# RWKV-6 recurrence and a token-mixing MLP on one core: twelve of the loads split into 120 and 8 partitions

## The chip, the cores and the metric

The kernel runs on 1 core of one Trainium2 chip. The metric is the device time of one execution in microseconds (us); lower is better. Before the change three runs gave 105.36, 105.78 and 107.31 us, median 105.78.

## What is computed

Inputs `r`, `k`, `v`, `w` have 4 batches, 8 heads, 768 tokens and 48 channels in float32; `u` is 8 x 48. The first stage is a recurrence per batch and head, the second a mixing of all tokens of a batch:

```
for t in range(768):
    cur = outer(u * k[t], v[t])
    y[t] = r[t] @ (state + cur)
    state = w[t][:, None] * state + outer(k[t], v[t])
x = y as (batch, 768, 8 * 48 = 384)
wq, wk = x @ w_q, x @ w_k                       # 384 -> 64
mixed = (wq @ wk.T / sqrt(64)) @ x
out = relu(mixed) @ w_out                       # 384 -> 384
```

## The kernel before

The work is cut into 12 units of 256 tokens, three for each batch (`unit(n, batch)`, L429). A unit holds two chunks of 128 tokens; the recurrence is done chunk by chunk as matrix products, and only the 48 x 48 states are carried from chunk to chunk.

**Loads.** For each unit SyncE's queue (SP) issues one transfer of 384 KB for each of `w`, `k` and `r` (tiles `wg`, `kg`, `rg`), and for `v` (`vg`) in the first nine units; the last batch (`WHOLE`, L233) gets its `v` by four transfers of another shape (`vw`, `load_whole`, L296). `load` (L291) lays two neighbouring tokens in one partition: 128 partitions, in each 8 heads times 96 floats, so 8 runs of 384 bytes a partition. Each kind has a ring of four buffers (`RINGS`, L257). The weights of the second stage come by three transfers in the middle of the loads.

**A unit's steps.** ScalarE (ACT) takes the logarithm of `w` into `lw` (L453); GpSimd (POOL) or ACT casts `kg` and `rg` to bf16 (`k`, `r`, L463); POOL casts `vg` (`v`, L556). TensorE (PE) sums the logarithms with a triangular matrix (`CM`, `cw`), ACT makes the exponentials `ep` and `en` (L491, L496). PE transposes `k` and `r`; a copy of the former is `ks`, and VectorE (DVE) multiplies to `RT` (L531) and `qT` (L522), POOL or DVE to `KT` (L539). PE puts `v` into token order (`vp`, with the permutation `PM`; a copy is `VB`). PE makes the products of a chunk (`A`), DVE masks them (`AM`, L608), POOL makes the diagonal term `Vd` (L588), PE the state (`sn`; `SB`, L654) and the outputs (`yi`, `ya`), DVE joins them to `X` (L712). Transposed (`XT`) they go into the products `QK`. At the end of a batch PE makes `T`, `mx` and `fp`, copies give `TS`, `MX` and `os`, and SP stores (L824). All matmuls have line L240.

**The order of the work.** A class `Plan` holds all steps. Each has a fixed rank (`RANK`, L165); `order()` (L80) lets each engine's steps stand in the order of their ranks and merges the engines' lists by planned durations, with which it also assigns PSUM banks. A load's issue, its time on the wire and its landing are planned by `plan.dma` (L73), called for loads at L441. SP's steps stay in the order of their ranks whatever happens on the chip, and so do the other engines' steps; waits go by semaphores. The transfers use eight landing semaphores in turn, and a transfer waits for the one that used its semaphore before, eight transfers earlier.

With the order in the program, the loads of SP from the eleventh on are: kg n3, wg n3, rg n2, wg n4, vg n2, vg n3, rg n3, kg n4, kg n5, three weights, rg n4, wg n5, rg n5, vg n4, kg n6, wg n6, vg n5, wg n7, kg n7, rg n6, kg n8, vg n6, vg n7, vg n8, wg n8, rg n7, rg n8, rg n9, and the rest ("kg n3" is the tile `kg` of unit 3).

Of the kernel before, what the change touches and what calls it, by code (L numbers as in the profile page):

```python
# [17 lines left out]
def view(t, off, dims, p0=0, pn=128):  # L18

    base = t[ds(p0, pn), ds(off, 1)]  # L20
    return dataclasses.replace(base, ap=[list(base.ap[0])] + [list(d) for d in dims])
# [12 lines left out]
class Plan:  # L34
# [12 lines left out]
    def add(self, key, engs, fn, after=(), buf=None, reads=(), lag=None, mode=0, behind=None):  # L47
        e = next(iter(engs)) if len(engs) == 1 else next(self.alt, "")
        e = e if e in engs else next(iter(engs))
        if lag is None:  # L50
            lag = 260 if e == "E" else 80
        s = dict(key=key, engs=engs, eng=e, dur=engs[e], fn=fn, lag=lag, mode=mode, rank=0,
                 behind=behind, after=list(after), buf=buf, reads=list(reads), i=len(self.steps))
        if buf is not None:
            if buf.filler is None:
                buf.filler = s
                s["fill"] = buf.kind
                if behind is None:
                    s["behind"] = self.last.get(buf.kind)
                if buf.kind in self.rings:  # L60
                    self.last[buf.kind] = s
            else:
                s["fill"] = None
                if behind is None:
                    s["behind"] = buf.filler
        else:
            s["fill"] = None
        for b in reads:
            b.readers.append(s)
        self.steps.append(s)  # L70
        return s
# [133 lines left out]
def kernel(  # L205
# [12 lines left out]
    nc = tc.nc  # L218
    B, H, S, D = r.shape
    C = 128  # L220
    U = 2 * C
# [3 lines left out]
    D2 = 2 * D  # L225
# [5 lines left out]
    N = B * NU  # L231

    WHOLE = (3,)  # L233

    SHIFT = 25
    MU = -SHIFT * math.log(2.0) / C
# [11 lines left out]
    def const(shape, dtype, name):  # L248
# [15 lines left out]
        QK=(2, QW, BF16), TS=(2, DM, BF16), vw=(2, NCH * DM, F32))  # L264
    if not WHOLE:
        del RINGS["vw"]
# [21 lines left out]
    gv = const([C, 1], F32, "gv")  # L288
    gk = const([C, 1], F32, "gk")

    def load(b, i, tl, ap):  # L291
        nc.sync.dma_start(  # L292
            out=view(tl, 0, [[D2, H], [1, D2]]),
            in_=ap[b, :, ds(i * U, U)].rearrange("h (p j) d -> p h (j d)", j=2))

    def load_whole(b, q, tl):  # L296
        n_ = H // 2 * NCH
# [62 lines left out]
    def ring(kind):  # L360
        b = Buf(kind)
        b.tile = tiles[kind][used[kind] % RINGS[kind][0]]
        used[kind] += 1
        return b
# [7 lines left out]
    def at(b, dtype=F32):  # L372
        x = PS[:, ds(b.bank * 512, 1024 if b.kind == "w" else 512)]
        return x if dtype == F32 else x.bitcast(dtype)

    def copies(cols, half=False, by=False):

        return {"A": (270 if by else 170) + int(cols * 0.835),
                "D": (210 if by else 150) + int(cols * (0.523 if half else 1.045))}

    def copy(e, o, i, by=None):
        if e == "A":
            if by is None:
                nc.scalar.copy(o, i)  # L384
            else:
                nc.scalar.activation(o, i, ACT.Copy, bias=0.0, scale=by)
        else:
            x = nc.vector if e == "D" else nc.gpsimd
            if by is None:
                x.tensor_copy(o, i)  # L390
            else:
                x.tensor_scalar_mul(o, i, by)
# [36 lines left out]
    def unit(n, batch):  # L429
        b, i = divmod(n, NU)  # L430
# [4 lines left out]
        fine = each if split else both  # L435
        whole = b in WHOLE

        g = {}
        for name, ap in (("wg", w), ("kg", k), ("rg", r)) + (() if whole else (("vg", v),)):
            g[name] = ring(name)  # L440
            g[name + "L"] = plan.dma((name, n), 570, 1190 + 250 * (n == 0 and name == 'kg') + 250 * (n > 2),  # L441
                                     lambda e, ap=ap, x=g[name].tile: load(b, i, x, ap),
                                     buf=g[name])[1]
        if whole and i == 0:
            batch["vw"] = ring("vw")
# [41 lines left out]
        for cs in fine:  # L487
# [11 lines left out]
            x = add(("ep", n, cs[0]), {"A": 190 + int(w_ * 0.837)}, f_ep, [cws], ep, [cw])  # L499
# [27 lines left out]
        for cs in fine:  # L527
# [8 lines left out]
            def f_KT(e, cs=cs, n4=n4):  # L536
# [3 lines left out]
            x = add(("RT", n, cs[0]), {"D": 150 + int(n4 * C * 0.524)}, f_RT,  # L540
                    [rTs] + [eps[c] for c in cs], RT, [rT, ep])
# [43 lines left out]
        for cs in fine:  # L585
# [5 lines left out]
            x = add(("Vd", n, cs[0]), {"P": 185 + 646 * len(cs)}, f_vd, [VBs, dds], Vd, [VB, dd])  # L591
# [22 lines left out]
        for cs in ([(0,)] if final else fine):  # L614
# [4 lines left out]
            x = add(("kb", n, cs[0]), {"E": 225 * len(cs)}, f_kb, [KTs[c] for c in cs], kb, [KT])  # L619
# [4 lines left out]
            x = add(("kd", n, cs[0]), copies(DM * len(cs), True, True), f_kd, [x], kd, [kb])  # L624
# [46 lines left out]
        for side in sides:  # L671
# [5 lines left out]
            def f_yi(e, side=side, cs=cs, first=not yis[cs[0]]):  # L677
# [3 lines left out]
                for hp in range(NP):  # L681
# [4 lines left out]
            x = add(("yi", n, *side[0]), {"E": 54 * len(side) + 60 * bool(yis[cs[0]])}, f_yi,  # L686
                    [RTs[c] for c in cs] + [oldss[c] for c in cs] + yis[cs[0]], ys[cs[0]],
                    [RT] + [olds[c] for c in cs], mode=1)
# [18 lines left out]
        for p, cs in enumerate(each if end else both):  # L707
# [42 lines left out]
            if not end:  # L750
                def f_qk(e, f_wk=f_wk, f_wq=f_wq):
# [3 lines left out]
                x = add(("QK", n), copies(384), lambda e, qk=qk: copy(  # L755
                    e, QK.tile[:, ds(i * QS, 384)], at(qk)[:, ds(0, 384)]), [qs], QK, [qk])
# [79 lines left out]
    for n in range(N):  # L836
        if n % NU == 0:
            batch = {"k": [], "q": [], "x": []}
        unit(n, batch)
# [42 lines left out]
```

## Time and profile before

| what | value |
|---|---|
| median of 3 runs | 105.78 us (105.36 to 107.31) |
| the profiled execution: span from its first to its last instruction | 104.4 us |
| the profiled execution's own time beyond the span | not recorded; the median is 1.4 us above the span |
| mean granted TensorE clock | 0.984 |
| read from HBM, written to it | 19.66 MB, 4.72 MB |
| loads of 384 KB: median time from issue to landing, wg, kg, rg, vg | 5.4, 5.9, 5.9, 5.8 us |

The page of the profile has the busy time of each engine (PE TensorE matmuls, PEld its weight loads, DVE VectorE, ACT ScalarE, POOL GpSimd, SP SyncE's queue), the span in 40 slices, the DMA queues (q1 is SP's queue of loads and stores, q8 and q14 fetch instructions), the chain of work that ended last, and the costliest groups of instructions. "A <- B" in the waits says that A stood idle until B had finished. In a timeline a line has start, duration, engine, line, operation, out<-in, and in brackets the engine's idle time before it and what ended it. A wait for several semaphores is put down to the one that came last by the profile.

### The profile page before, as it was taken

What the parts mean: (1) busy time and instruction counts of PE and PEld (TensorE: products, weight loads), DVE (VectorE), ACT (ScalarE), POOL (GpSimd) and SP (SyncE); (2) the same over time, 40 slices, a digit from 0 to 9 for tenths busy, and PEclk for the clock granted to TensorE, in tenths of its full rate; (3) what the DMA queues carried; (4) which work ended last, traced back from release to release, by engine and by line L of the source; (5) the groups of instructions that cost most, each with busy time, mean ns of one, the idle gap of its engine ahead of it and who ended that gap; (6) DMA issues with size and microseconds to landing.
All of it is one profiled execution on the core that took longest, in us unless ns stands there. A gap on an engine that the chain in (4) does not pass through costs nothing.

```text
span 104.4 us, 3964 instructions
## 1 busy us (share of the span) xinstructions
PE 93.2 (89%) x1651; PEld 69.4 (66%) x1652; DVE 84.4 (81%) x140; ACT 80.6 (77%) x122; POOL 69.3 (66%) x80
## 2 busy tenths in 40 slices
PE   5999899766998999999999899999999998999910
PEld 2356488544777786767886776887888596866500
DVE  6669996995789979979999889999899699695320
ACT  6348988759879869999999886899897954855830
POOL 6607666979998828959995699999975973000000
PEclk9999999999589999999999999999999999999999
DMA  1999999999999988999999799999993056004791
GB/s 26 296 324 325 325 318 234 309 290 237 301 342 295 246 228 206 303 254 243 310 294 256 195 264 276 244 179 172 292 349 137 0 220 238 0 9 181 295 359 72
DMA packets 56803, 24.65 MB, mean 236 GB/s; under 512 B 54480, under 2 KB 55632, under 8 KB 56784
## 3 DMA queue, kind: packets, MB, share of 16 engines
q1 hardware_dynamic: 56224, 24.19, 84.3%
q8 instruction: 13, 0.21, 0.8%
q10 hardware_dynamic: 560, 0.20, 0.7%
q14 instruction: 6, 0.05, 0.1%
HBM read 19.66 MB, written 4.72 MB: 234 GB/s over the span
## 4 chain that ended last, share of the span: by engine, by line
PE 74%; DMA 6%; POOL 5%; DVE 5%; issue 3%; ACT 2%; SPq 1%; POOLq 0%; DVEq 0%
PE PS L240 74%; DMA vg<-in_v_dram 6%; DVE KT L539 2%; POOL KT L539 2%; POOL v L556 2%; POOL Vd L588 1%; ACT ep L491 1%; ACT MX L396 1%; DVE RT L531 1%; DVE AM L608 1%; SPq L292 1%; DVE qT L522 1%; ACT os L384 0%; DVE Z L306 0%; POOL r L463 0%
## 5 line engine op out<-in xcount | busy, mean ns | idle before, releaser
L608 DVE TENSOR_TENSOR AM<-PS,US 128x1024 bf16<-128x1024 f32 x24 | 29.3, 1219 | 3.4 <-PE PS L240 3.2
L539 POOL TENSOR_TENSOR KT<-ks,en 128x1024 bf16<-128x1024 bf16 (+1 forms) x11 | 20.5, 1864 | 3.6 <-DVE ks L390 3.4
L588 POOL TENSOR_TENSOR Vd<-VB,dd 128x768 bf16<-128x768 bf16 (+1 forms) x14 | 18.1, 1294 | 1.3 <-ACT dd L384 1.2
L712 DVE SCALAR_TENSOR_TENSOR X<-PS,gx,Vd 128x768 bf16<-128x768 f32 (+1 forms) x13 | 12.4, 952 | 2.8 <-POOL Vd L588 1.4
L240 PEld LDWEIGHTS <-KT 48*128 48x128 bf16 (+1 forms) x272 | 10.9, 97 | 5.2 <-issue 2.4
L496 ACT ACTIVATE en<-PS 128x1024 bf16<-128x1024 f32 (+1 forms) x14 | 12.6, 898 | 2.0 <-PE PS L240 2.0
L491 ACT ACTIVATE ep<-PS 128x1024 bf16<-128x1024 f32 (+1 forms) x14 | 12.7, 919 | 1.3 <-ACT XT L384 0.6
L453 ACT ACTIVATE lw<-wg 128x768 bf16<-128x768 f32 x12 | 10.2, 848 | 4.5 <-DMA wg<-in_w_dram 4.4
L240 PE MATMUL PS<-wo,MX 128*128 128x384 bf16 x72 | 13.3, 326 | 0.0
L463 POOL CAST k<-kg 128x768 bf16<-128x768 f32 x11 | 9.0, 825 | 3.3 <-DMA kg<-in_k_dram 3.3
L384 ACT COPY os<-PS 128x768 f32<-128x768 f32 (+1 forms) x13 | 8.6, 680 | 2.5 <-PE PS L240 2.2
L463 POOL CAST r<-rg 128x768 bf16<-128x768 f32 x9 | 7.5, 835 | 4.3 <-DMA rg<-in_r_dram 2.3
L556 POOL CAST v<-vg 128x768 bf16<-128x768 f32 x9 | 7.4, 825 | 3.6 <-DMA vg<-in_v_dram 3.6
L240 PE MATMUL PS<-RT,KT 48*128 48x128 bf16 x192 | 9.7, 221 | 0.0
L240 PEld LDWEIGHTS <-MX 128*128 128x128 bf16 x72 | 6.5, 98 | 4.1 <-issue 0.3
L531 DVE TENSOR_TENSOR RT<-PS,ep 128x1024 bf16<-128x1024 bf16 (+1 forms) x14 | 8.4, 607 | 0.8 <-PE PS L240 0.5
L396 ACT ACTIVATE MX<-PS 128x768 bf16<-128x768 f32 (+1 forms) x11 | 8.2, 755 | 0.7 <-PE PS L240 0.6
L522 DVE TENSOR_TENSOR qT<-PS,ks 128x1024 bf16<-128x1024 bf16 x12 | 8.2, 681 | 0.4 <-issue 0.4
L240 PE MATMUL PS<-Z 128*128 128x512 bf16 x20 | 7.4, 511 | 1.2 <-DVE uT L309 1.2
L384 ACT COPY XT<-PS 128x768 bf16<-128x768 bf16 (+1 forms) x9 | 6.9, 765 | 2.0 <-PE PS L240 2.0
L240 PE MATMUL PS<-ID,r 128*128 128x128 bf16 x96 | 7.7, 226 | 0.4 <-POOL r L463 0.3
L240 PE MATMUL PS<-VB,AM 128*128 128x48 bf16 x192 | 7.9, 184 | 0.1
(83 smaller groups left out, 201.1 us busy)
## 6 DMA issues: line engine op xcount, KB each, us to landing
wg<-in_w_dram SPq DMA_DIRECT2D x12, 384.0 KB, 5.4
kg<-in_k_dram SPq DMA_DIRECT2D x12, 384.0 KB, 5.9
rg<-in_r_dram SPq DMA_DIRECT2D x12, 384.0 KB, 5.9
vg<-in_v_dram SPq DMA_DIRECT2D x9, 384.0 KB, 5.8
out_dram<-os SPq DMA_DIRECT2D x9, 384.0 KB, 3.0
vw<-in_v_dram SPq DMA_DIRECT2D x4, 288.0 KB, 6.2
out_dram<-os SPq DMA_DIRECT2D x5, 192.0 KB, 2.7
wof<-in_moe_w_out_dram SPq DMA_DIRECT2D x1, 576.0 KB, 5.4
```

The lines of the kernel that those rows point to most:

```text
L240: return nc.tensor.matmul(o, l, rr, start=start, stop=stop, skip_group_check=True, is_transpose=trans)
L384: nc.scalar.copy(o, i)
L453: nc.scalar.activation(view(lw.tile, 0, [[64, H], [512, 2], [1, D]]), view(g["wg"].tile, 0, [[D2, H], [D, 2], [1, D]]), ACT.Ln, bias=0.0, ...
L463: op(view(o.tile, 0, [[64, H], [512, 2], [1, D]]), view(g[src].tile, 0, [[D2, H], [D, 2], [1, D]]))
L491: nc.scalar.activation(view(ep.tile, cs[0] * NP * EW + 66, [[EW, NP * len(cs)], [-65, 2], [1, 64]]), at(cw)[:, ds(cs[0] * 512, w_)], ACT.E ...
L496: nc.scalar.activation(en.tile[:, ds(cs[0] * 512, w_)], at(cw)[:, ds(cs[0] * 512, w_)], ACT.Exp, bias=0.0, scale=-1.0)
L531: nc.vector.tensor_tensor(view(RT.tile, cs[0] * 512, [[C, n4], [64, 2], [1, 64]]), view(at(rT, BF16), cs[0] * 512, [[C, n4], [64, 2], [1, ...
L539: x.tensor_tensor(KT.tile[:, cols], ks.tile[:, cols], en.tile[:, cols], ALU.mult)
L556: v16s = add(("v16", n), {"P": 826}, lambda e: nc.gpsimd.tensor_copy(view(v16.tile, 0, [[D, H], [DM, 2], [1, D]]), view(g["vg"].tile, 0, [ ...
L588: nc.gpsimd.tensor_tensor(Vd.tile[:, cols], VB.tile[:, cols], view(dd.tile, cs[0] * H, [[1, len(cs) * H], [0, D]]), ALU.mult)
L608: AMs[c] = add(("AM", n, c), {"D": 1221}, lambda e, c=c, A=A: nc.vector.tensor_tensor(view(AM[c].tile, 0, [[C, 8], [1, C]]), view(at(A), 0 ...
L712: nc.vector.scalar_tensor_tensor(view(X.tile, (2 * i + c0) * DM, [[DM, nc_], [1, DM]]), view(at(y), 0, [[512, nc_], [1, DM]]), gx, view(Vd ...
```

## The change

In the loads of `kg` and `rg` of units 3 to 8, twelve loads, partitions 0 to 119 go by one transfer and partitions 120 to 127 by a second one issued right behind it on the same queue. The bytes and the destination are the same; the planner's durations and ranks are unchanged, and so is the order of all other instructions on every engine. SP issues 12 transfers more, and the casts that read these tiles wait for both transfers.

```diff
+    CUT = [(0, 120), (120, 8)]
...
-    def load(b, i, tl, ap):
-        nc.sync.dma_start(
-            out=view(tl, 0, [[D2, H], [1, D2]]),
-            in_=ap[b, :, ds(i * U, U)].rearrange("h (p j) d -> p h (j d)", j=2))
+    def load(b, i, tl, ap, cut):
+        rows = ap[b, :, ds(i * U, U)].rearrange("h (p j) d -> p h (j d)", j=2)
+        for p0, pn in cut:
+            nc.sync.dma_start(out=view(tl, 0, [[D2, H], [1, D2]], p0=p0, pn=pn),
+                              in_=rows[p0:p0 + pn])
...
+            cut = CUT if name in ("kg", "rg") and 3 <= n <= 8 else [(0, 128)]
             g[name + "L"] = plan.dma((name, n), 570, 1190 + 250 * (n == 0 and name == 'kg') + 250 * (n > 2),
-                                     lambda e, ap=ap, x=g[name].tile: load(b, i, x, ap),
+                                     lambda e, ap=ap, x=g[name].tile, cut=cut: load(b, i, x, ap, cut),
                                      buf=g[name])[1]
```

## Prediction

> **What bounds the kernel now.** I read the page first, then the chain of waits in order of time, then the waits, then the DMA view in two stretches, then the timeline of SP and of POOL, and last the landings themselves. Unit n is one of the 12 units of 256 tokens; "kg n3" is the load of keys of unit 3.
>
> From the page (part 1; part 2, the GB/s row; part 3):
>
> ```profile
> PE 93.2 (89%) x1651; PEld 69.4 (66%) x1652; DVE 84.4 (81%) x140; ACT 80.6 (77%) x122; POOL 69.3 (66%) x80
> ...
> GB/s 26 296 324 325 325 318 234 309 290 237 301 342 295 246 228 206 303 254 243 310 294 256 195 264 276 244 179 172 292 349 137 0 220 238 0 9 181 295 359 72
> ...
> q1 hardware_dynamic: 56224, 24.19, 84.3%
> q8 instruction: 13, 0.21, 0.8%
> ```
>
> PE is the busiest engine, and the loads are not idle either: 325 GB/s up to the sixth slice (13 us), then mostly 170 to 310. From there on a second queue, q8, is at work: 13 instruction packets of 16,384 bytes; in the trace's packet records they start at 13.47, 20.13, 27.63, 36.02, 43.01, 50.99, 56.10, 63.81 us and later, and take 0.88 to 0.96 us each up to there. The chain of waits, in order of time (start, us, what):
>
> ```profile
> 17.55 5.83 DMA vg<-in_v_dram
> ...
> 23.53 0.83 POOL v L556
> ...
> 24.41 1.89 PE PS L240 x40
> ...
> 35.38 13.19 PE PS L240 x243
> ...
> 58.37 0.05 POOL r L463
> ```
>
> The end is set by a load (vg n2) until 24.4 us, and by PE nearly without a break after it. What PE waits for (who, for whom: us in total, times, longest):
>
> ```profile
> PE PS L240 <- POOL v L556: 1.6, 1, 1.6
> PE PS L240 <- DVE KT L539: 0.9, 2, 0.4
> PE PS L240 <- POOL r L463: 0.3, 1, 0.3
> ```
>
> So a change of the loads can win little more on PE than these waits, while a loss has no such limit. SP's timeline shows how the loads are paced (start, us):
>
> ```profile
> 9.27 1.11 SPq L292 DMA_DIRECT2D wg<-in_w_dram  x1
> 10.42 2.52 SPq L292 DMA_DIRECT2D kg<-in_k_dram  x2
> 12.99 2.10 SPq L292 DMA_DIRECT2D wg<-in_w_dram  x1
> 15.13 1.21 SPq L292 DMA_DIRECT2D rg<-in_r_dram  x1
> 16.45 1.05 SPq L292 DMA_DIRECT2D wg<-in_w_dram  x1
> 17.55 2.49 SPq L292 DMA_DIRECT2D vg<-in_v_dram  x2
> 20.08 2.03 SPq L292 DMA_DIRECT2D rg<-in_r_dram  x1
> ```
>
> SP issues one load behind the other without a gap; an issue takes 1.05 to 1.25 us, which is the time that a load needs on the wire, and 2.0 to 2.9 us where a q8 packet starts. Each load ends with 16 counts on its landing semaphore, one for each of 16 engines; the trace has their times (us):
>
> ```
> load    issued   15th count   16th count   behind
> rg n1     8.08        12.87        13.00     0.13
> kg n2    10.42        15.39        16.47     1.08   q8 packet at 13.47
> kg n3    11.80        16.59        17.58     0.99
> wg n3    12.99        18.64        18.78     0.14
> vg n2    17.55        22.55        23.38     0.83   q8 packet at 20.13
> vg n4    31.69        36.75        38.48     1.73   q8 packet at 36.02
> kg n7    39.61        44.64        45.95     1.31   q8 packet at 43.01
> rg n8    50.96        56.47        58.23     1.76   q8 packets at 50.99, 56.10
> ```
>
> One engine of 16 falls about 1 us behind with each instruction packet. A load is complete only with its 16th count, and SP's next issue stretches until that engine has room, so all 16 lose the time: kg n3 to wg n3 the other 15 advance by 18.64 - 16.59 = 2.05 us, the late one by 1.20.
>
> **The change part by part.** A load has 128 rows x 8 heads, 1024 runs of 384 bytes, so 64 runs, or 8 rows, for each of 16 engines. Twelve loads (kg and rg of units 3 to 8) become 120 rows and 8 rows. 120 rows are 15 full shares: one engine is given nothing of the large transfer. The 8 rows are 64 runs more for others. No compute instruction is added or moved on PE, DVE, ACT or POOL, and SP's loads keep their order, with 12 issues more.
>
> (1) The spared engine. If it is the late one, each cut takes one share, 1.2 us, off its queue, against 0.88 to 0.96 us that a q8 packet puts on. kg n3 sits right behind the packet at 13.47, rg n3 to kg n5 behind that at 20.13, rg n4 and n5 behind 27.63, kg n6 behind 36.02, kg n7 to n8 behind 43.01, rg n7 and n8 behind 50.99. Then 2.10 - 1.15 = 0.95 us at 12.99 goes, and most of the later stretches. The trace names no engine. What speaks for the late one: in the seven loads that land between 7 and 14.2 us, before any packet, one count is already last each time by 0.12 to 0.16 us, as the engine would be that is handed its share last; and 8 rows left at the end of 128 are the last share.
> [...]
>
> (2) The added pieces. 64 runs at 1.2 us / 64 = 18.75 ns each: over 8 engines 8 runs, 0.15 us; over 16 engines 0.08; on one engine 1.2 us. The nearest row with small pieces is wkf, 24 runs of 256 bytes an engine, whose 15th count comes 0.19 us after wqf's (29.22 - 29.03), less than 24 x 18.75 ns = 0.45, so no fixed cost shows. I take 0.15 (kept: 0 to 0.25) a cut on the engines that carry it: 1.8 us over twelve. On engines that are not the late one it fills time in which they wait (0.85 us around 17 us).
>
> (3) SP. 12 more issues of 0.43 (rg at 27.18) to 0.57 us: 5 to 7 us of SP's time. A cut pair then costs at least 0.86 to 1.1 us of issue, under the 1.15 that the wire needs, so it hides; were that cover gone, it would cost up to 0.1 us a pair. Behind it on SP stand only loads and, from 71 us, stores. The loads use 8 landing semaphores in turn, so a transfer also waits for the one 8 before; with three cuts in a row that is 5 loads back, about 6 us, and issue to landing is 5.4 to 5.9 us (page, part 6). A wait there stops an issue while some three loads are still queued: 0 on the path.
>
> (4) The consumers. Twelve casts wait for one semaphore more. Where POOL stands idle, its sequencer takes 0.04 + 0.08 us before the cast (chain, 58.25 to 58.37); where POOL runs back to back nothing. I take 0 (kept: 0 to 0.3).
>
> Path, if the late engine is spared. vg n2 lands at 23.38 - 0.95 + 0.15 = 22.58. POOL, from its timeline:
>
> ```profile
> 20.62 2.13 POOL L539 TENSOR_TENSOR KT<-ks,en 128x1024 bf16<-128x1024 bf16 x1 [0.21 <-ACT ks L384]
> 23.53 0.82 POOL L556 CAST v<-vg 128x768 bf16<-128x768 f32 x1 [0.78 <-DMA vg<-in_v_dram]
> ...
> 58.37 0.83 POOL L463 CAST r<-rg 128x768 bf16<-128x768 f32 x1 [2.04 <-PE PS L240]
> ```
>
> KT ends at 22.75, so the cast of v starts then: 0.78 earlier, and PE's start at 24.41 follows (it waited 1.59). From 23.5 to 33.5 us POOL is back to back and from 35.4 to 58 us PE is, so the 0.78 is carried and nothing is added, though vg n4 and kg n7 land earlier too. The cast of rg n8 at 58.37 is put down to PE, but its semaphore's 16th count came at 58.23, 1.76 after the 15th: it was the load. Landing earlier, it frees PE's wait of 0.32 at 59.26 and the 0.2 before 63.55 (PEld <- POOL KT): 0.5. At 80.40 PE starts 0.05 us after the cast of rg n11 (landed 79.47); that load hangs on SP's queue, which has by then gained several us, so the shift holds. What is late next is PE itself. Sum: -0.78 - 0.5 = -1.28, so -1.3 us. The profile gives only its span, 104.4 us, and the median of the runs is 105.78, 1.4 above it for what lies around; 105.78 - 1.3 = 104.5. This case alone: 103.6 (DVE KT's 0.9 won too) to 105.4 (only 0.4 stays).
>
> **The rivals.**
> *The late engine carries the added pieces.* Then nothing is relieved and it gets 0.15 us more with each cut. vg n2 is late by 0.15 (one cut before it); rg n8, with twelve, by 1.8, and PE, which already waits for that cast, waits for all of it: 105.78 + 1.8 = 107.6 (106.3 to 108.8 with 0.05 to 0.25 a cut). It decides from rg n8 on; for it speaks that no row names an engine. Chance 0.20.
> [...]
> *The change does not do what it says for the late engine:* it neither loses its share nor gains pieces. The pieces then fill the others' waiting time: 105.8. Against it speaks that 15 shares of 8 must leave one engine free, and one in 16 is late. Chance 0.12.
> *Loads bound more than the chain shows:* PE wins all of its 1.59 at 24.41, the 0.9 at DVE KT and 0.5 at 59 to 63.5: 3.0, so 102.8. Against it: KT on POOL ends at 22.75 whatever lands. Chance 0.10.
>
> **How the numbers follow.** The forecast has the remaining 0.58. A measurement of this kernel tells about 2%, 2.1 us, from no change (the three runs spread over 1.95), so the bounds are 103.66 and 107.9. Faster: 0.10 x 0.9 + 0.58 x 0.1 = 0.15. Slower: 0.20 x 0.5 = 0.10. Same: 0.75. The range 103.3 to 107.7 leaves out most of the last rival and half of the first: about 2 in 10. The likeliest case has 103.6 to 105.4 for its own.
>
> **What would show it.** Right: SP's issue of wg n3 near 13 us takes about 1.2 instead of 2.10; wg n3's 16th count near 17.8; vg n2 at about 22.6 and the cast of v at 22.8; PE's wait there near 0.8; the GB/s row in slices 7 to 23 mostly near 300; POOL's 2.04 before rg n8's cast gone. Wrong: the cut loads' last counts still 1 us behind, stretches of 2 us kept, or loads landing 0.15 us later per cut up to 1.8 at rg n8. The size is wrong if PE's order of work stalls anew between 35 and 58 us.

## The result and the profile after

The changed kernel takes 109.74 us (median of 4 runs, 109.03 to 112.69) against 105.89 us in the same session; the ratio is 1.034, 95% interval [1.028, 1.039]. That is slower, above the forecast of 104.5 and above the range's end of 107.7. The profiled execution took 109.03 us of its own time, its span is 107.3 us (104.4 before): 2.9 us more. In the profiles of experiments 1 and 8 and of the first twin of experiment 10 the profiled execution was one of the slower ones of its kernel; the verdicts are from the timed runs.

From the page of the kernel after, parts 1, 2 and 3:

```profile
PE 93.3 (87%) x1651; PEld 68.9 (64%) x1652; DVE 84.6 (79%) x140; ACT 80.3 (75%) x122; POOL 70.2 (65%) x80
...
GB/s 34 299 316 324 325 292 236 253 309 240 229 296 231 213 236 231 293 215 233 265 271 260 271 269 320 288 149 198 273 359 119 6 105 341 0 0 149 272 358 113
...
q1 hardware_dynamic: 56308, 24.19, 87.7%
```

PE's work is the same, 93.3 us for 93.2. The bytes of q1 are the same too (24.19 MB), but its packets take 87.7% of a longer span for 84.3%: 0.877 x 107.3 = 94.1 us for 88.0, so the same bytes hold the engines 6.1 us longer. Slices 7 to 23 were to come near 300 GB/s and are mostly at 210 to 270. The chain, by engine:

```profile
PE 35%; DMA 22%; SPq 15%; POOL 10%; ACT 7%; DVE 4%; issue 4%; POOLq 0%; ACTq 0%
```

Before it was PE 74%, DMA 6%. In order of time, two loads of `r` stand in the middle of it now, where PE had run without a break:

```profile
21.49 2.15 POOL KT L542
23.65 0.83 POOL v L559
24.52 1.18 PE PS L241 x16
...
29.54 6.36 DMA rg<-in_r_dram
36.00 0.84 ACT r L466
36.89 0.64 PE PS L241 x8
...
44.48 6.18 DMA rg<-in_r_dram
50.69 0.76 POOL Vd L591
...
55.98 5.36 DMA rg<-in_r_dram
```

(Line numbers are 1 to 3 higher than before: the loads have L295, the casts L466 and L559.) PE's waits:

```profile
PE PS L241 <- POOL v L559: 2.5, 3, 1.0
PE PS L241 <- POOL k L466: 1.4, 4, 0.6
PE PS L241 <- DVE uT L311: 1.2, 1, 1.2
PE PS L241 <- POOL r L466: 0.8, 2, 0.5
```

v was one wait of 1.6 and is now three; k was 0.4, r 0.3. Why those casts are late is read on POOL's timeline, whose brackets name what ended its idle time. After:

```profile
26.99 0.82 POOL L466 CAST r<-rg 128x768 bf16<-128x768 f32 x1 [0.43 <-DMA rg<-in_r_dram]
27.75 0.83 POOL L559 CAST v<-vg 128x768 bf16<-128x768 f32 x1
28.81 0.83 POOL L466 CAST k<-kg 128x768 bf16<-128x768 f32 x1 [0.23 <-DMA kg<-in_k_dram]
30.73 0.83 POOL L466 CAST k<-kg 128x768 bf16<-128x768 f32 x1 [1.09 <-DMA kg<-in_k_dram]
...
61.48 0.83 POOL L466 CAST r<-rg 128x768 bf16<-128x768 f32 x1 [1.54 <-DMA rg<-in_r_dram]
```

The same casts before, without a bracket, so back to back:

```profile
26.38 0.82 POOL L463 CAST r<-rg 128x768 bf16<-128x768 f32 x1
27.14 0.83 POOL L556 CAST v<-vg 128x768 bf16<-128x768 f32 x1
27.91 1.62 POOL L463 CAST k<-kg 128x768 bf16<-128x768 f32 x2
```

The first cast of a cut load that waits, r at 26.99, is that of rg n3, the second cut load; the two casts of keys behind it are those of kg n4 and n5, the next two. (v of unit 3 is late because it stands behind the waiting cast of r.) Before these, a load that is not cut is late already: kg n2 landed at 17.45 (16.47 before), its cast came 0.98 us later, and POOL's work behind it moved with it. After, that cast and the product `KT` ahead of the cast of vg n2, and below them the same cast before:

```profile
17.57 0.82 POOL L466 CAST k<-kg 128x768 bf16<-128x768 f32 x1 [2.33 <-PE PS L241]
...
21.49 2.14 POOL L542 TENSOR_TENSOR KT<-ks,en 128x1024 bf16<-128x1024 bf16 x1
```

```profile
16.59 0.82 POOL L463 CAST k<-kg 128x768 bf16<-128x768 f32 x1 [1.77 <-DMA kg<-in_k_dram]
```

(The wait at 17.57 is put down to PE, but the load's last count came 0.12 us before the cast.) Where the time is lost, by stretches (stretch, length, busy us and count of each engine, TensorE clock, DMA share, GB/s), before:

```profile
24.40:38.00 13.60, 12.97 (x243) 10.48 (x242) 10.91 (x15) 11.35 (x17) 11.39 (x11) 0.87 1.05 285
38.00:52.00 14.00, 13.83 (x276) 10.44 (x273) 12.75 (x21) 13.30 (x18) 11.93 (x11) 1.00 0.96 251
52.00:66.00 14.00, 13.54 (x265) 10.25 (x262) 12.48 (x18) 12.12 (x21) 11.96 (x11) 1.00 0.99 260
66.00:104.00 38.00, 32.92 (x581) 25.63 (x577) 28.18 (x43) 26.66 (x46) 18.38 (x17) 1.00 0.61 183
```

and after:

```profile
24.40:38.00 13.60, 11.72 (x240) 9.26 (x240) 11.76 (x16) 10.40 (x15) 11.25 (x11) 1.00 1.13 242
38.00:52.00 14.00, 12.49 (x243) 9.02 (x241) 10.91 (x19) 12.13 (x17) 9.58 (x9) 1.00 1.05 242
52.00:66.00 14.00, 12.72 (x245) 9.97 (x245) 11.48 (x17) 11.57 (x16) 12.04 (x11) 1.00 1.08 275
66.00:104.00 38.00, 35.99 (x635) 27.60 (x633) 31.23 (x47) 29.19 (x50) 21.41 (x20) 1.00 0.65 187
```

PE has 35.99 - 32.92 = 3.07 us more left to do at 66 us, and the span is 2.9 us longer: the loss is made by then. In 24.4 to 38 us the loads bring 242 GB/s for 285 while the DMA engines are counted busier (1.13 for 1.05): not fewer transfers in flight, but slower ones (experiment 6 has the time of single packets). (The full clock there hid part of it: 240 matmuls took 11.72 us, 243 before 12.97.)

The counts on the landing semaphores (us; a cut load is complete with the later of its two last counts):

```
load     last count before   after (120 rows, 8 rows)   later by
kg n2              16.47     17.45 (not cut)              0.98
kg n3              17.58     18.73, 17.90                 1.15
vg n2              23.38     23.50 (not cut)              0.12
rg n3              25.81     26.54, 26.84                 1.03
kg n5              28.58     30.58, 30.57                 2.00
rg n5              35.33     38.96, 39.21                 3.88
kg n8              48.31     52.24, 51.50                 3.93
rg n8              58.23     61.08, 61.34                 3.11
```

The 120-row transfers leave 15 counts when they land and one as soon as they are issued, the 8-row ones 8. Read as one count an engine, 15 engines and 8 do the work. But a late engine is among the 15, so it was not spared: the 15th of these counts is 1.06 us (kg n3), 1.26 (kg n7), 1.17 (rg n6) and 1.00 (kg n8) behind the 14th, as the 16th was before, and the pieces of the same loads had all their counts by then.

### The profile page after: what moved, and what is told of

Read it like the earlier page. It is cut to its first block, busy times and chain, and to the rows that moved or that the text cites. A ratio compares the mean times of both kernels' runs of the same rounds, so it can differ in the third digit from the quotient of the medians.

```text
span 107.3 us, 3982 instructions
## 1 busy us (share of the span) xinstructions
PE 93.3 (87%) x1651; PEld 68.9 (64%) x1652; DVE 84.6 (79%) x140; ACT 80.3 (75%) x122; POOL 70.2 (65%) x80
## 3 DMA queue, kind: packets, MB, share of 16 engines
q1 hardware_dynamic: 56308, 24.19, 87.7%
## 4 chain that ended last, share of the span: by engine, by line
PE 35%; DMA 22%; SPq 15%; POOL 10%; ACT 7%; DVE 4%; issue 4%; POOLq 0%; ACTq 0%
PE PS L241 35%; DMA rg<-in_r_dram 17%; SPq L295 15%; POOL KT L542 6%; DMA wg<-in_w_dram 5%; DVE AM L611 2%; POOL Vd L591 2%; POOL v L559 2%; ACT QK L386 1%; ACT ks L386 1%; ACT en L499 1%; ACT ep L494 1%; ACT kd L388 1%; ACT r L466 1%; ACT MX L398 1%
## 5 line engine op out<-in xcount | busy, mean ns | idle before, releaser
L241 PEld LDWEIGHTS <-KT 48*128 48x128 bf16 (+1 forms) x272 | 10.4, 95 | 4.9 <-issue 2.2
L466 POOL CAST k<-kg 128x768 bf16<-128x768 f32 x11 | 9.1, 823 | 6.1 <-DMA kg<-in_k_dram 3.7
L466 POOL CAST r<-rg 128x768 bf16<-128x768 f32 x9 | 7.7, 864 | 5.1 <-DMA rg<-in_r_dram 2.8
L241 PE MATMUL PS<-ID,k 128*128 128x128 bf16 x96 | 7.4, 220 | 1.5 <-POOL k L466 1.4
L386 ACT CAST VB<-PS 128x768 bf16<-128x768 f32 x9 | 7.1, 793 | 1.8 <-PE PS L241 1.6
L241 PE MATMUL PS<-CM,lw 64*128 64x128 bf16 x192 | 7.9, 222 | 0.6 <-ACT QK L386 0.3
```

The costliest lines, as they stand in the source:

```text
L241: return nc.tensor.matmul(o, l, rr, start=start, stop=stop, skip_group_check=True, is_transpose=trans)
L466: op(view(o.tile, 0, [[64, H], [512, 2], [1, D]]), view(g[src].tile, 0, [[D2, H], [D, 2], [1, D]]))
```

## The experiments

Two theories to begin with. **Slower transfers** (theory L in the expectations): a transfer of 120 rows takes the engines longer than a whole load, whatever is spared. **The rivals**: the pieces or the additional issues and counts cost the time (T), or the uneven shares of the engines (I); or the late engine carries the pieces. From the fifth experiment on the first of them is told more sharply, as one of the *ways into SBUF* (P): which partitions a transfer covers sets its time, since engines that write to the same part of them hinder each other. The first half is what experiments 6 and 10 measure; the second is the author's supposition, as no record here names an engine. All ratios are to the kernel before, in runs of the same session.

**1. Another cut of the same size class: 112 and 16 rows.**

```diff
-    CUT = [(0, 120), (120, 8)]
+    CUT = [(0, 112), (112, 16)]
```

> The twelve loads are cut into 112 and 16 rows in place of 120 and 8: as many transfers as in the changed kernel, but 7 and 1 rows on each of 16 engines, so no engine carries more than before. Theory T, the count of transfers costs (each added piece takes the engines or SP's queue some 0.3 us whatever it holds): about 109 us, rg n8 landing about 3 us later than before. Theory I, the imbalance costs (8 engines carry 9 rows for 8, one none): about 105.9 us, rg n8 at 58 us.

Measured: 1.027 [1.018, 1.035]. All 16 engines have work in both transfers here (16 counts each), none is spared, and the loss is about that of 120 and 8. So the loss needs neither a spared engine nor uneven shares: theory I falls, T still stands.

**2. The 120 rows alone**, in units 4 to 8 (ten loads). The last 8 partitions are not loaded; they keep what an earlier unit left.

```diff
-    CUT = [(0, 120), (120, 8)]
+    CUT = [(0, 120)]
...
-            cut = CUT if name in ("kg", "rg") and 3 <= n <= 8 else [(0, 128)]
+            cut = CUT if name in ("kg", "rg") and 4 <= n <= 8 else [(0, 128)]
```

> In kg and rg of units 4 to 8 only rows 0 to 119 are loaded, by one transfer; rows 120 to 127 keep an older unit's values, so that part of the computation is changed. No transfer is added and 15 engines carry what they carried before. Theory T and theory I: 105.9 us or up to 1 less, and the late engine still late, since the spared one is another. A third theory, L (a 120-row transfer is slow in itself): 108 to 109.5 us.

Measured: 1.018 [1.008, 1.027]. With less to read, no second transfer, no further issue and no further wait, the kernel is slower. The last counts of kg n7, rg n6 and kg n8, which are issued one behind the other, are at 47.34, 48.98 and 50.89: 1.6 to 1.9 us a transfer. The rival that only pieces, issues or counts cost falls.

**3. The pieces alone**: whole loads, and behind each of the twelve a piece of 8 rows into a scratch tile that nobody reads.

```diff
+    SCR = [const([C, HW], F32, "scr")] + [16 * (x % 8) for x in range(12)]
...
-        for p0, pn in cut:
+        for p0, pn in [(0, 128)]:
             nc.sync.dma_start(out=view(tl, 0, [[D2, H], [1, D2]], p0=p0, pn=pn),
                               in_=rows[p0:p0 + pn])
+        if len(cut) > 1:
+            nc.sync.dma_start(out=view(SCR[0], 0, [[D2, H], [1, D2]], p0=SCR.pop(), pn=8),
+                              in_=rows[0:8])
```

> The twelve loads stay whole, and behind each a transfer of 8 rows goes to a scratch tile that nothing reads: the added piece without the cut. Theory T and theory I: about as the changed kernel, 109 to 109.7 us (8 engines carry 9 rows for 8, and a piece more each). Theory L: 105.9 to 106.5 us.

Measured: 0.993 [0.988, 0.997]. Twelve pieces more on SP and on the wire cost nothing; rg n8 landed at 57.37 (58.23 before). Whether they even help was tried again:

> The kernel with whole loads and twelve scratch pieces of 8 rows once more, since it came out at 0.9925 of before. If the pieces help: 0.985 to 0.998. If that was chance: an interval around 1.00 or above.

Measured: 1.003 [0.998, 1.008]. They neither help nor hurt; the 0.993 was not repeated.

**4. Halves.** `CUT = [(0, 64), (64, 64)]`.

> The twelve loads are cut into two halves of 64 rows: 4 rows on each of 16 engines twice, balanced. Theory T: about 109 us, like the uneven cut, since the count is the same. Theory I: 105.9 us. Theory S, that a small piece costs since it takes a full place in SP's queue while it feeds the engines little: halves feed them more, so between, about 107 us.

Measured: 1.047 [1.039, 1.055], the worst of the cuts, though each half is 4 rows for each of 16 engines (an estimate from the 64 rows; the `vw` loads of before, 64 partitions too, leave 16 counts each). The halves follow each other at 0.8 to 1.0 us, so 1.6 to 2.0 for a load that takes 1.2 whole.

**5. The price of each shape by itself.** The kernel before, with 56 more load steps (the expectation says 57) of various shapes behind its last store, where nothing else moves (the span is longer by these).

> The kernel before, with 57 further load steps behind its last store, on SP's queue, with nothing beside them: runs of equal shapes, whose spacing of last landings is the time of one on the wire. Its time is the kernel's plus theirs. Theory P (the shape of the share: when a transfer is not 128 rows, the engines' rows fall so that several engines meet on the same way into SBUF): 128 rows 1.2 us, 120 rows 1.5 to 1.8, 112 rows 1.3 to 1.6, 64 rows at 0 or at 64 about 0.85, 64 rows at 32 about 0.6, a whole load with 8 rows more 1.35. Theory K (only 15 engines in place of 16): 120 rows 1.2, 64 rows 0.6 wherever they lie. Theory Q (nothing but the traffic in the kernel makes them slow): all in proportion to their rows, 120 rows 1.2 or less.

**6. Which property sets it?** The same with all transfers of a kind reading the same first rows, only the number of rows and the partitions that they go to changed.

> Again load steps behind the last store of the kernel before, spacing of last landings for one: now all read the same rows of HBM for a shape (from row 0 on) and only the partitions that they write differ, and 60 rows bring 15 engines at 4 rows each. Theory P (ways into SBUF): 64 rows to partitions 32 to 95 0.60 us, to 0 to 63 1.0; 60 rows to 32 to 91 0.60 (15 engines harmless), to 0 to 59 about 1.0; 120 rows 1.5 at 0 and at 8. Theory K (15 engines in place of 16 is slow): 60 rows at 32 clearly over 0.60, 0.75 or more. Theory R (the rows read in HBM make the difference): 64 rows alike at both places.

Measured in both, from last count to last count of transfers that follow each other (us a transfer; the first and the last of a kind, in which the kinds overlap, are left out; `e5_shapes` is experiment 5, `e7_shapes2` experiment 6):

```
rows   to partitions    e5_shapes      e7_shapes2               1.2 us x rows / 128
128    0 to 127         1.19 to 1.20   1.18 to 1.21             1.20
120    0 to 119         1.43 to 1.49   1.43 to 1.50             1.13
120    8 to 127         1.56           1.45 to 1.49             1.13
112    0 to 111         1.27 to 1.68   -                        1.05
96     0 to 95          1.16 to 1.21   -                        0.90
64     0 to 63          0.92 to 1.06   0.99 to 1.08             0.60
64     64 to 127        0.98 to 1.07   -                        0.60
64     32 to 95         0.56 to 0.62   0.59, 0.59, 0.61, 1.09   0.60
60     32 to 91         -              0.56 to 0.62             0.56
60     0 to 59          -              1.00 to 1.09             0.56
120+8  the cut          1.83, 1.83, 2.41 a pair                 1.20
128+8  8 to scratch     1.43 (mean) a pair                      1.28
```

(The 1.09 is the one ahead of the transfers to partitions 0 to 63, and the 2.41 the last of its kind. For 128 rows in `e5_shapes` the row has the five loads at the end; those at the start, right behind the kernel's last stores, came at 1.21 and 1.76.)

SP's timeline of the second of them shows the same as a pace: issues behind 120-row transfers, and the last two, behind whole loads.

```profile
131.47 1.42 SPq L841 DMA_DIRECT2D rg<-in_k_dram  x1
132.93 1.40 SPq L841 DMA_DIRECT2D kg<-in_v_dram  x1
134.38 1.37 SPq L841 DMA_DIRECT2D vg<-in_r_dram  x1
...
147.81 1.16 SPq L841 DMA_DIRECT2D wg<-in_w_dram  x1
149.01 1.13 SPq L841 DMA_DIRECT2D rg<-in_k_dram  x1
```

64 rows to partitions 32 to 95 take 0.60 us, the same 64 rows to partitions 0 to 63 take 1.0: neither the bytes, nor the number of runs, nor what is read decides, but where it goes. Fifteen engines are not slower as such either, if 60 rows go by fifteen as 120 do (15 counts in the changed kernel; for 60 rows it is an estimate, four rows an engine): 60 rows to partitions 32 to 91 take 0.57, and theory K falls with that. And moving the 120 rows by 8 partitions leaves them at 1.5. Since nothing else runs here, it is not the kernel's other traffic (Q falls). Theory P had the sizes nearly; only 64 rows to partitions 0 to 63 were expected at 0.85 and took 1.0.

The trace's packet records show the same of single packets. Each carries one run of 384 bytes. Median times in `e7_shapes2`, taken while the middle transfers of a kind land:

```
128 rows, 64 rows to 32 to 95, 60 rows to 32 to 91     22 ns each
120 rows to 0 to 119, to 8 to 127                      27 and 22 ns, a quarter of them 33 ns or more
64 rows to 0 to 63, 60 rows to 0 to 59                 42 and 44 ns
```

And in the kernel, of the packets between 38 and 52 us, over 30 ns take: 1% before, 22% after the change, 25% with the 120 rows alone, 24% with the halves, 3% with the twelve pieces. Single packets take longer, then, and which ones do goes with the rows and the partitions of the transfer.

Why the place decides is not shown, as no trace here names an engine: the rows say which transfers are slow (64 rows to partitions 0 to 63 with 1.0 us, 120 rows with 1.5), not what holds their packets up.

**7. Ten cuts instead of twelve** (units 4 to 8).

```diff
-            cut = CUT if name in ("kg", "rg") and 3 <= n <= 8 else [(0, 128)]
+            cut = CUT if name in ("kg", "rg") and 4 <= n <= 8 else [(0, 128)]
```

> The change for units 4 to 8 alone: ten loads of 120 rows with a piece of 8 behind, where the run with 120 rows alone had the same ten without the pieces (ratio 1.018). Theory P or L (the 120-row transfer is the cost, the piece none): 1.02 to 1.03, as much as 10/12 of the change's 1.034 at most. If the pieces have a price of their own behind a 120-row transfer: above the run without them by more than its interval, 1.028 or more.

Measured: 1.041 [1.029, 1.052]; rg n8 at 61.49. Without the pieces it was 1.018 (experiment 2), so behind a 120-row transfer a piece has a price of its own, the second of the two outcomes named. Without the cuts of unit 3 the loss is not smaller (the intervals overlap), so it is not made in the early stage that the forecast counted on.

**8. Twice as many pieces**: whole loads, and a scratch piece behind all 24 loads of w, k, r and v of units 3 to 8.

> All loads whole; a scratch piece of 8 rows, which nothing reads, behind each of 24 loads (w, k, r, v of units 3 to 8) in place of twelve, which gave 0.9925. If the pieces themselves shorten the standstills that the late engine causes: 0.985 to 0.993. If that gain was the chance position of the instruction packets, with 0.15 us for each piece on 8 engines: 0.995 to 1.02.

Measured: 1.026 [1.016, 1.036], above both expectations. 24 pieces do cost, where 12 were free. At 0.23 us a piece (table) 2.8 us of wire time found room, 5.5 did not.

**9. Is the way to vg n2 the thing to shorten?** The kernel before with the loads of vg n2 and wg n4 exchanged in SP's order (`x["rank"], z["rank"] = z["rank"], x["rank"]`), so that v lands one load earlier.

> The kernel before with one change, no load cut: the loads of v of unit 2 and of w of unit 4 swap places on SP's queue, so that the load on which PE's longest wait hangs lands one load, about 1.0 us, earlier. By the prediction's path step (POOL is free at 22.75 in place of 23.53): -0.7 us, 0.993. If the load of w, then as much later, becomes the wait: 1.00 or above.

Measured: 1.023 [1.017, 1.029], a miss. v was cast at 22.65 and PE's wait for it fell to 0.5, but another took its place. ACT's timeline, and PE's waits:

```profile
24.37 0.84 ACT L453 ACTIVATE lw<-wg 128x768 bf16<-128x768 f32 x1 [3.08 <-DMA wg<-in_w_dram]
```

```profile
PE PS L240 <- ACT ep L491: 2.4, 1, 2.4
...
PE PS L240 <- POOL v L556: 0.5, 1, 0.5
```

wg n4 lands at 24.29 now (22.34 before), ACT stands idle for 3.08 us before its logarithm, and PE waits 2.4 us for the exponentials. Not all of the 1.95 us is the exchange: the load's 15th count came 1.34 us later than before, and its 16th stood 1.60 us behind that, where it was 0.98. So what vg n2 alone would win, with no other load later, stays open. The loads are handed out closely: one load later is paid at once by whoever needs it. That is also why the kernel has so little room for longer loads.

**10. The deciding pair.** In ten loads (k and r of units 4 to 8) two transfers of 64 rows instead of one of 128; the first to the tile, the second to a scratch tile. The twins differ in one number, `p0`: both transfers go to partitions 32 to 95, or both to 0 to 63. Both read the first 64 rows of the unit, so the k and r that the unit computes with are changed.

```diff
+        for dst in ([tl, SCR.pop()] if len(cut) > 1 else []):
+            nc.sync.dma_start(out=view(dst, 0, [[D2, H], [1, D2]], p0=32, pn=64), in_=rows[0:64])
```

> In the loads of k and r of units 4 to 8 (ten loads) each whole load becomes two transfers of 64 rows, both to partitions 32 to 95 (the second to a scratch tile that nobody reads); both read the first 64 rows of the unit, so the k and r that the unit computes with are not the reference's. Two transfers and the bytes of a whole load, as in the halves cut (64 to partitions 0 to 63, 64 to 64 to 127: 1.047 for twelve). Theory of the ways into SBUF (which partitions a transfer covers sets its time): 64 rows to partitions 32 to 95 took 0.56 to 0.64 us behind the last store, so a pair takes 1.2 us as the whole load does: rg n8 lands at 57.5 to 58.5, time 104.8 to 106.5, ratio 0.99 to 1.01. Rival (any second transfer on the queue, or a transfer of other than 128 rows, costs by itself): the same loss as in the twin kernel with partitions 0 to 63, 1.03 to 1.05.

> The twin: the same ten loads, the same rows, the same scratch tiles, two transfers of 64 rows each, both to partitions 0 to 63; the k and r that the unit computes with are not the reference's. Theory of the ways into SBUF: 64 rows to partitions 0 to 63 took 1.0 us behind the last store, so a pair takes 2.0 us where the whole load takes 1.2, 8 us more over the ten loads; the halves cut had 0.8 to 1.0 us a half and 1.047 over twelve, so 1.03 to 1.05 here, 109 to 111 us, rg n8 landing at 61 to 63. Rival (the number of transfers or of rows alone): the same time as the twin with partitions 32 to 95.

Measured: to partitions 32 to 95 0.993 [0.985, 1.000], to 0 to 63 1.078 [1.062, 1.094]. The windows of the first

```profile
38.00:52.00 14.00, 13.83 (x277) 10.57 (x278) 12.75 (x21) 13.31 (x17) 12.26 (x11) 1.00 1.03 270
```

and of the second:

```profile
38.00:52.00 14.00, 11.56 (x173) 8.53 (x172) 8.73 (x16) 10.09 (x15) 8.66 (x8) 0.88 1.11 214
```

Same transfers, rows, bytes, issues and counts: 270 GB/s and 277 matmuls against 214 and 173. (The granted clock of 0.88 may be part of PE's lower count.) The six halves of kg n7, rg n6 and kg n8 follow each other at 0.56 to 0.65 us in the first and at 1.06 to 1.28 in the second, and in this stretch 1% and 42% of the packets take over 30 ns. rg n8 (its half in the tile) landed at 57.70 and 65.28. So ten loads split in two cost nothing by themselves, and the partitions that a transfer covers decide. The second was expected at 1.03 to 1.05, after the halves cut, whose halves followed at 0.8 to 1.0 us. That it is worse since both its halves press on the same partitions, while in the halves cut one half follows on the other half of them, is argued, not shown.

**All together**: the wire time that each edit adds by the table, and what the kernel lost by its ratio:

```
kernel                        added by the table (us)    measured (us)
64 and 64 to 32..95, ten      10 x (2 x 0.60 - 1.2) = 0      -0.8
pieces, 12                    12 x 0.23 = 2.8                -0.8 and +0.3
120 rows alone, ten           10 x 0.3 = 3.0                 +1.9
pieces, 24                    24 x 0.23 = 5.5                +2.7
the cut 120+8, ten            10 x 0.63 = 6.3                +4.3
the cut 120+8, twelve         12 x 0.63 = 7.6                +3.6
64 and 64 to 0..63, ten       10 x (2 x 1.0 - 1.2) = 8.0     +8.2
halves, twelve                12 x (2 x 1.0 - 1.2) = 9.6     +5.0
```

(Of 112 and 16 rows the 16 were not measured by themselves.) More added time is more loss on the whole, but neither in strict order nor in proportion. Twelve cuts lost no more than ten (their intervals overlap). The halves lost less than the table says: at the 0.8 to 1.0 us at which they followed each other in the kernel, 4.8 to 9.6 us were added. And up to about 3 us is partly or wholly hidden. That fits the loads' own standstills before (SP's issues of 2.0 to 2.9 us), which added wire time can fill, but which edit fills them how far was not separated. No kernel here beats the one before: of the two just under 1, one came out at 1.003 when it was repeated, and the other does not load half of the rows that it needs.

## Why the prediction was wrong, point by point

- **What bounds the kernel.** PE, with one wait on vg n2, was read rightly, and so was that "a loss has no such limit". What was missed is how close the other casts stood to their loads: rg n3's cast had 0.57 us to spare (landing 25.81, start 26.38), and that of kg n4 0.58 (27.33, 27.91).
- **(1) The spared engine.** This is the step that failed first. "120 rows are 15 full shares" was worked out from the rows, with no run behind it; the changed kernel has 15 counts for them. But the share was taken at the 1.2 us of the whole load. Measured by itself a 120-row transfer takes 1.43 to 1.56 us, on average 1.5. The gain of "one share, 1.2 us" a cut wasn't there either: in five of the cut loads the last of 15 counts is 1.0 to 1.3 us behind, so a late engine is among the 15. Which engine falls behind stays open. The premise that it is one and the same engine is doubtful: the pieces of rg n4, rg n5 and kg n6 have a count 1.0 to 1.15 us behind the one before, the other nine 0.1 to 0.55, though kg n3, kg n7, rg n6 and kg n8 among these nine have a late count in the large transfer. If all pieces go to the same eight engines, which no record shows, the late one was among them in some loads and not in others.
- **(2) The added pieces.** "0.15 (kept: 0 to 0.25) a cut" is near to what a piece adds behind a whole load (0.23), and twelve of those cost nothing (0.993, 1.003). Behind 120 rows the pair takes 1.83 for 1.2: +0.63 a cut is the term that was mis-sized, 0.3 of it for the 120 rows and 0.33 for the piece. The 0.15 in the sum for vg n2, and in the first rival's 1.8, took the 8 rows to go over 8 engines, which no run had shown; the changed kernel has 8 counts for a piece, but no run shows 0.15. Why a piece adds 0.33 there and 0.23 behind a whole load was not looked into.
- **(3) SP.** The 12 issues hid, as forecast: experiment 3 has them all at no cost. That the issue of the cut pairs grew with the wire, and not the other way round, is argued from this, not shown by itself.
- **(4) The consumers** at 0: no run sets it apart, but a row bounds it. rg n8's 8 rows had their last count at 61.34 and the cast started at 61.48, 0.14 later, as it was before (58.23, 58.37).
- **The path.** The sum counted -0.78 us at vg n2 and -0.5 us at rg n8; neither came. Instead of vg n2 at 22.6 it landed at 23.50, and the 2.10 us issue near 13 us became 0.76 behind two of 1.22 and 1.10, with 1.77 next: nothing won. Nor was POOL free at 22.75 for the cast of v: since kg n2 was 0.98 late, `KT` ended at 23.63, so an earlier vg n2 would have found POOL busy. That kg n2 is late is hardly chance, though it is a whole load ahead of the first cut: in the profiles of the three kernels that cut kg n3 behind it, it lands at 16.89, 17.45 and 17.64, in all eleven others at 16.38 to 16.70. kg n3 is issued at 11.99, so both are under way together; how the one delays the other was not looked into. The signs named as wrong are there: last counts 1 us behind, loads late up to rg n8.
- **The rivals.** "The late engine carries the added pieces" had the right sign, and the place (it grows with each cut), at half the size: 1.8 us at rg n8 (3.0 with its 0.25 a cut), measured 3.1; 107.6 us (108.8), measured 109.74. Its mechanism is not what made the loss: in kg n3, kg n7, rg n6 and kg n8 the pieces were complete before the late count, and twelve pieces behind whole loads cost nothing. "Loads bound more than the chain shows" was priced as a gain only; the loads do bound more, as a loss (DMA 22% of the chain, 6% before).
- **The range** left out that a transfer of other than 128 rows could be slower itself. The trace of before had one row that hinted at it and was not used: the vw loads (64 partitions, 288 KB) stand 1.5 to 2.2 us on SP, whole loads of 384 KB 1.05 to 1.25. It is no more than a hint, as the runs of vw have 192 bytes instead of 384, and instruction packets (63.81 and 68.60 us) run during three of the four issues.

## What to carry to other kernels

The price of a transfer was not its bytes here (128 rows 1.20 us, 120 rows 1.5): ask which partitions it fills, and look in the trace for a transfer of that shape before a share of a whole load is taken as its price. Where all 128 partitions can be filled at once, leave them whole (1.20 us, against 1.83 as 120 and 8 rows); where 64 must do, 32 to 95 took 0.60 us and 0 to 63 took 1.0. Before adding to a queue that already feeds a busy engine, list for each consumer how long its load had lain there; here the next two had 0.6 us, and that was gone after two cuts.

## What the runs showed of the hardware that was not expected

- 120 rows take longer than 128: 1.5 us for 1.20, and 96 rows (1.16 to 1.21) as long as 128.
- The same 64 rows take 0.60 us to partitions 32 to 95 and 1.0 to 0 to 63; the same with 60 rows (0.57, 1.0). A packet of 384 bytes takes 22 ns in the one and 42 to 44 in the other.
- Twelve pieces of 8 rows behind whole loads were free in the kernel (0.993 and 1.003), though each adds 0.23 us where nothing else runs.
